# Reordering both hand-written task lists of a fused attention and state-space kernel

## The chip, the cores and the metric

The kernel runs on one core of one Trainium2 chip. The metric is the device time of one execution in microseconds (us). TensorE is PE in the profile (its weight loads are the row PEld), VectorE is DVE, ScalarE is ACT, GpSimd is POOL and SyncE is SP; SP, POOL and, for a few loads, ACT issue the DMAs.

## The reference, cut to what matters

Two layers work on the same input `x` (2048 positions, 640 channels, bf16), and a gate mixes them.

```python
x = A_x
g = _sigmoid((x * gate_w).sum(-1, keepdims=True))
a = _A_ref(x, A_wqkv, A_wo)
b = _B_ref(x, B_A_re, B_A_im, B_B_re, B_B_im, B_C_re, B_C_im, B_log_dt, B_Dskip)
return g * a + (1 - g) * b
```

`_A_ref` is attention of 32 heads of 20 channels over a dilated window: each position sees itself and seven earlier ones at a distance of 2. `_B_ref` builds a convolution kernel `K` of 2048 taps for every channel, as a sum of 192 complex exponentials whose rates come from the parameters (`A`, `B`, `C`, `log_dt`), and convolves `x` with it by a Fourier transform.

## The kernel before, in words

**Tasks and lists.** The work is cut into tasks (class `Task`, L104). `Plan.add` (L123) names a task, the engines that may do it and what it depends on. There are two plans: `main` has 1258 tasks, `tail` 304. Nothing is scheduled at run time: `Plan.order` (L140) reads the sequence from the string in `ORDER` (L54). Every number there is the step from one task's index to the next, and a letter behind it names the engine where the task is not done by the first engine that it allows; most evictions may be done by ScalarE ("A", the default) or by VectorE ("D"). `Plan.emit` (L152) writes the instructions in this sequence and ties each one to the instruction before it on the same engine (L169), so the list fixes the program order of every engine and of every DMA queue, and also the order in which buffers are handed out. The switch of ScalarE's function table (L160) is written where the list changes between exp/ln and sin/atan tasks.

**What is outside the lists.** `SSMParams.build` (from L535) issues the first loads before any task, always in the same sequence on SP: `cre`, `cim`, a first transposed quarter of `x` (`xl[0]`), the Q part of the attention weights (`wl[0]`), `aim`, `are`, the K part and the V part (`wl[1]`, `wl[2]`), then the other three quarters of `x`.

**Projections.** Tasks `late0` to `late59` (L268 to L307) project `x` to Q, K and V: 4 chunks of 512 positions, 3 kinds, 5 pieces. In a chunk, the first five numbers are Q, the next five K, the last five V: `late0` is Q, `late7` is K and `late14` is V of the first chunk. One is 5 matmuls of 512 columns (2 in `late..`, 3 in `late..b`, L284) into a PSUM tile `tb`, of which there are two; `lev..` evicts it (L476 on ScalarE, L478 on VectorE). A third projection therefore waits for the eviction of the first. Attention's `gat` (L424) and `wo` (L448) matmuls use the same two tiles.

**Parameters.** Tasks `wr`, `t0`, `wi`, `tau`, `act_..`, `stt_..`, `mk0` to `mk9` turn the parameters into ten pieces, mostly on VectorE with 960 elements a row (L593 to L630) and some on ScalarE (L602, L658 to L666). The pieces are stored to DRAM (`sp0` to `sp9`, SP, L623) and loaded back as `L` (L734): `L0S` on SP and `L0G` on POOL for the first of ten chunks, `L1` to `L9` on SP for the others. The last piece in both lists is `mk6`.

**Kernel generation.** For chunks 0 to 9: `arg` matmuls (L769), `act` on ScalarE (sine L784, exponential L786; 15 a chunk), `pq` products on VectorE (L806, L808) and `kmm` matmuls (L824). `act00000` is the first of the activations, `pq00` the first of the products. After chunks 4 and 9, `own`, `other` (L872 ff.) spread half of the kernel, which goes through DRAM (`xst`, `xld`) and comes back as `kc` for the first transforms `f1` and `fk`; `fu` transforms `x` (L1272, L1291).

**Attention.** Eight blocks of 256 positions: `prod` (VectorE, L343), `lg`, `max`, `neg`, `exp`, `sum`, `at`, a round trip of the probabilities through DRAM (`ast`, `asb`), `pv` (VectorE, L417), `gat`, `oT`, `wo`, `ga`. `halo` copies (L478) carry the last keys of a block to the next.

**Tail.** The second plan does the second transform step (`fp`, evicted by `sp`), the products (`ta`, `tc`, `Y` on VectorE), the inverse (`inv`, evicted by `cp`; `yp`), the mixing (`tt`, `mx`, `st`) and the stores.

Of the kernel before, what the change touches and what calls it, by code (L numbers as in the profile page):

```python
# [40 lines left out]
def _attn_consts():  # L41
# [10 lines left out]


ORDER = {"main": (  # L54
# [37 lines left out]
), "tail": (  # L92
# [8 lines left out]
)}  # L101


# [1269 lines left out]
```

## Time and profile before

| what | value |
|---|---|
| three runs | 324.24, 324.82, 326.2 us (median 324.82) |
| span of the profiled execution | 324.0 us, 11730 instructions |
| busy PE, DVE, ACT | 278.8, 293.5, 281.6 us |
| bytes moved by DMA | 45.65 MB, mean 141 GB/s |

The profiled execution's time is not listed apart from its span. The page counts an engine as busy while it works on an instruction; what is left of the span is idle. Views that answer for a stretch of the span ("windows") give the busy time of each engine in it and, behind x, the instructions. A row of the timeline begins with the start and the time taken; in square brackets at its end stands how long the engine sat idle before it, and what ended that. A "q" behind an engine's name is its queue of DMA issues.

### The profile page before, as it was taken

What the parts mean: (1) busy time and instruction counts of PE and PEld (TensorE: products, weight loads), DVE (VectorE), ACT (ScalarE), POOL (GpSimd) and SP (SyncE); (2) the same over time, 40 slices, a digit from 0 to 9 for tenths busy, and PEclk for the clock granted to TensorE, in tenths of its full rate; (3) what the DMA queues carried; (4) which work ended last, traced back from release to release, by engine and by line L of the source; (5) the groups of instructions that cost most, each with busy time, mean ns of one, the idle gap of its engine ahead of it and who ended that gap; (6) DMA issues with size and microseconds to landing.
All of it is one profiled execution on the core that took longest, in us unless ns stands there. A gap on an engine that the chain in (4) does not pass through costs nothing. (4 is left out here: it accounts for less than half of the span.)

```text
span 324.0 us, 11730 instructions
## 1 busy us (share of the span) xinstructions
PE 278.8 (86%) x5109; PEld 168.9 (52%) x5134; DVE 293.5 (91%) x408; ACT 281.6 (87%) x425; POOL 55.8 (17%) x87
## 2 busy tenths in 40 slices
PE   0599998999989999999999979889999999996750
PEld 0145443454545545546554544457677776665740
DVE  4888989899998999999999999798999899999891
ACT  1489578999989999999999999799997599997890
POOL 8500027501100000111112202050100000000062
PEclk9998999999999999999999997799999999999995
DMA  8997356642313102467774977144771493963056
GB/s 212 341 223 223 121 172 150 147 96 85 82 39 98 48 7 74 79 166 252 183 183 99 196 160 145 42 125 90 232 270 40 123 320 93 207 127 56 2 141 187
DMA packets 48698, 45.65 MB, mean 141 GB/s; under 512 B 28591, under 2 KB 42483, under 8 KB 48647
## 3 DMA queue, kind: packets, MB, share of 16 engines
q1 hardware_dynamic: 42524, 27.82, 33.4%
q0 software_dynamic: 5216, 16.39, 19.9%
q8 instruction: 40, 0.66, 0.9%
q10 hardware_dynamic: 906, 0.69, 0.7%
q14 instruction: 12, 0.09, 0.1%
HBM read 28.25 MB, written 14.01 MB: 130 GB/s over the span
## 5 line engine op out<-in xcount | busy, mean ns | idle before, releaser
L284 PE MATMUL tb<-bufA 128*128 128x512 bf16 x275 | 74.4, 400 | 6.2 <-DMA bufA<-in_A_wqkv_dram 2.9
L784 ACT ACTIVATE big<-ar 128x740 bf16<-128x740 int16 (+1 forms) x72 | 56.0, 852 | 2.2 <-PE ar L769 1.5
L786 ACT ACTIVATE big<-ar 128x848 bf16<-128x848 f32 x60 | 50.3, 918 | 3.4 <-PE ar L769 3.2
L769 PE MATMUL ar<-Rarg,L 64*128 64x212 bf16 (+4 forms) x600 | 47.5, 255 | 6.5 <-ACT big L784 2.7
L284 PEld LDWEIGHTS <-bufA 128*128 128x128 bf16 x300 | 32.5, 122 | 35.8 <-issue 13.2
L343 DVE TENSOR_TENSOR prod<-qr,kr 128x2048 bf16<-128x2048 bf16 x40 | 47.9, 1220 | 0.9 <-PE lg L349 0.8
L417 DVE TENSOR_TENSOR pv<-vc,asb 128x2048 bf16<-128x2048 bf16 x40 | 47.5, 1217 | 0.2 <-PE tb L424 0.2
L769 PEld LDWEIGHTS <-L 64*128 64x128 bf16 x600 | 22.5, 95 | 35.5 <-issue 32.5
L806 DVE TENSOR_TENSOR pt<-big 128x1024 bf16<-128x1024 bf16 x48 | 32.1, 701 | 1.4 <-PE kps L824 0.8
L824 PE MATMUL kps<-qq,pt 128*32 128x21 bf16 (+1 forms) x2560 | 27.9, 175 | 2.8 <-issue 2.6
L824 PEld LDWEIGHTS <-pt 128*32 128x32 bf16 (+1 forms) x2560 | 23.5, 92 | 11.5 <-issue 9.6
L448 PE MATMUL tb<-wo_sb,oTm 128*128 128x320 bf16 x160 | 27.8, 307 | 0.0
L476 ACT ACTIVATE sp_u<-fp 128x640 bf16<-128x640 f32 x29 | 22.4, 883 | 2.1 <-PE fp L1039 2.1
L476 ACT ACTIVATE sp_k<-fp 128x640 bf16<-128x640 f32 x30 | 22.7, 878 | 1.0 <-PE fp L1039 0.8
L424 PE MATMUL tb<-pv,ind 128*64 128x512 bf16 (+1 forms) x192 | 22.3, 355 | 0.6 <-ACT oTm L476 0.4
L337 POOL DMA_DIRECT2D vc<-vS x16 | 11.6, 728 | 64.0 <-DVE pv L417 57.8
L808 DVE TENSOR_TENSOR qq<-big 128x1344 bf16<-128x1344 bf16 x24 | 21.2, 883 | 0.0
L1039 PEld LDWEIGHTS <-PHI 128*128 128x128 bf16 x160 | 15.6, 97 | 8.1 <-issue 1.5
L448 PEld LDWEIGHTS <-oTm 128*128 128x128 bf16 x160 | 14.7, 99 | 7.8 <-issue 2.8
L160 ACT ACT_TABLE_LOAD x14 | 18.0, 1283 | 0.3
L1157 POOL DMA_DIRECT2D out_dram<-ot x14 | 7.8, 562 | 54.1 <-DVE ot L1139 54.1
L476 ACT ACTIVATE qr<-tb 128x512 bf16<-128x512 f32 (+1 forms) x22 | 10.8, 514 | 6.9 <-PE tb L284 6.9
(152 smaller groups left out, 500.9 us busy)
## 6 DMA issues: line engine op xcount, KB each, us to landing
vc<-vS POOLq DMA_DIRECT2D x16, 327.5 KB, 5.4
vS<-prj POOLq DMA_DIRECT2D x4, 640.0 KB, 5.8
gaS<-ga SPq DMA_DIRECT2D x8, 320.0 KB
Usb<-in_A_x_dram POOLq DMA_DIRECT2D x8, 320.0 KB, 5.2
gaF<-gaS SPq DMA_DIRECT2D x8, 320.0 KB
bufA<-in_A_wqkv_dram SPq DMA_DIRECT2D x3, 800.0 KB
Sprm<-pc SPq DMA_DIRECT2D x10, 240.0 KB
L<-Sprm SPq DMA_DIRECT2D x38, 60.0 KB
```

Of the source, the lines that this page charges most:

```text
L284: nc.tensor.matmul(ppf, self.wq[:, which, kt, e::5], self.xT[:, c0 // 1024, kt, c0 % 1024:c0 % 1024 + SC], start=(kt == 0), stop=(kt == NK ...
L343: nc.vector.tensor_tensor(b[e][:], self.qr[:, sc % NRB, e, :].unsqueeze(1).to_broadcast([128, W, C]), win(self.kr[:, sc % NRB, e, :], 0, W ...
L417: nc.vector.tensor_tensor(o, vw, b["asb"][:].unsqueeze(2).to_broadcast(sh), ALU.mult)
L424: nc.tensor.matmul(b["op", e][64 * a:64 * a + 64, 0:n, :], ind[:, 32:96], b["pv", e][:, w, a, 0:n, :], start=(w == 0), stop=(w == 3), skip ...
L448: nc.tensor.matmul(apf[:, :320], b["oT"][:, e, i * 128:(i + 1) * 128], wo_sb[:, e, hf * 320:(hf + 1) * 320], start=(e == 0), stop=(e == 4))
L476: nc.scalar.activation(o, i, ACT.Identity)
L769: nc.tensor.matmul(ar[:, g2, a0:a0 + ncol], L[rows, gv, sb, l0:l0 + 128], R[rows, c0:c0 + ncol], start=True, stop=True, tile_position=(64 ...
L784: nc.scalar.activation(d_[:, :, s0 * QW:s1 * QW], ar[:].bitcast(I16)[:, :, 0:2 * (s1 - s0) * QW:2], ACT.Sin, scale=SCL)
L786: nc.scalar.activation(dst[:, gp::2].rearrange("p g s n -> p g (s n)"), ar[:, :, 0:2 * EW], ACT.Exp)
L806: nc.vector.tensor_tensor(pt[:, :, k, :], gg[:, :, ::-1] if k else gg, e1, ALU.mult)
L808: nc.vector.tensor_tensor(qq[:], trg[:, :, KI:].rearrange("p a (v m) -> p a v m", v=2), exq[:, :, KI:].unsqueeze(2).to_broadcast([128, 32, ...
L824: nc.tensor.matmul(kps[32 * g:32 * g + 32, h ^ (g // 2), NM * ql:NM * ql + NM], pt[rows, k, v, :], qq[rows, k, v, :], start=(g not in star ...
```

## The change

Only the strings in `ORDER` differ. The tasks, what they compute, their dependencies and the loads ahead of the lists are the same. The diff, cut to the head and the end of each list:

```diff
 ORDER = {"main": (
-    "52 -52 3 -2 3 7 -6 -3 51 -47 6 -5 1 7 -6 45 10 1 2 -1 2 1 -14 1 -43 75 -31 -47 79 -13 -62 76 -65 52 -49 3 -15 62 -55 "
...
-    "-652 1D 640 14 -13D -640 648 -647 1 652D -13 1 -639 1 2 -1D 2 567 -566D 651 1D -651 646 1 1 1 -53 1D 45 1 -25 1D"
+    "94 1 1 -23 -71 80 1 1 -10 1D -75 1 3 7 -8 3 1 54 1 2 1 1 -3D -51 1 119 1 1 -55 -71 1 5 -4 18 -5 -18 11 1 30 33 1 -56 66 "
...
+    "-73 74 -20D 17 10 1D 11 1D -11 1D -12 -642 1 1 1 1 655 1D -65 -589 1 -2 591 49 1 -638 1 565 53 1 -23 1"
 ), "tail": (
-    "0 7 -6 1 1 1D 1 1D 5 -3 4 1 2 1 -7 5D 6 6 8 1D -25 7 124 -114 11 -20 1 2 19 -1 -9 -8 19 1 -10 -9 1 7 2 -5 1 20 1 -14 "
...
+    "0 3 1D 1 1 3 -2 1 2D -9 10 23 -21 23 -24D 2D 6 1 14 2 -7 -13 14 -16 1 2D 4 -20 21 3 1 5 1 5 2 -1 2 -13 -4 1 4 14 1 -25 "
...
```

Read as names, the head of `main` is, engine by engine (a task of the projections' second part, "b", is left out):

| engine | before | after |
|---|---|---|
| PE | late0, 4, 5, 1, 12, 8, 7, 9, 2 | late14, 7, 10, 3, 4, 26, 9, 13, 0 |
| DVE | wr, t1, t0, wr, wi, wi, dtc, tau, near_x1, xl | wi, lev7, wr, t0, wr, t1, wi, dtc, lev3, xl |
| ACT | act_xl, act_ax, act_xa, lnd, lev0, lev4 | lev14, lev10, act_xl, lev4, act_xa, lev26 |
| SP, later | sp9, sp6, L0S, L1, ast0 | sp6, sp9, L1, L0S, ast0 |

(`wr`, `wi`, `tau` and `near_x1` name more than one task; the first `wi` is `cre` times `bim`.) Up to and with `mk6` VectorE's list holds the same tasks before and after, and in addition `lev7`, `lev3` and `prod02` after.

Evictions and copies of `main` that may go either way, ScalarE / VectorE:

| | before | after |
|---|---|---|
| projections (lev) | 49 / 11 | 45 / 15 |
| halo copies | 1 / 6 | 7 / 0 |
| oT | 18 / 6 | 13 / 11 |
| ga | 22 / 10 | 26 / 6 |
| fin | 7 / 3 | 8 / 2 |
| first transforms f1, fk, fu | 34 / 11 | 35 / 10 |

In the tail the counts stay (sp 59 / 5, cp 12 / 8), while three sp and two cp evictions change places each way. The number of table switches in the list is 14 in both.

81 rows, old and new, of the table ORDER are left out of this document.

## The prediction

> **What bounds the kernel now.** I read the page's engine sums first, then the stretches of the span, then the first 65 us of the timeline.
>
> ```profile
> span 324.0 us, 11730 instructions
> PE 278.8 (86%) x5109; PEld 168.9 (52%) x5134; DVE 293.5 (91%) x408; ACT 281.6 (87%) x425; POOL 55.8 (17%) x87
> ```
>
> ```profile
> 4.47:39.84 35.37, 27.77 (x181) 13.67 (x184) 31.70 (x33) 22.61 (x38) 8.34 (x11) 0.95 0.84 235
> 51.24:324.00 272.76, 240.47 (x4867) 150.25 (x4884) 251.74 (x355) 250.63 (x372) 41.00 (x66) 0.97 0.52 129
> 61.50:324.00 262.50, 232.12 (x4784) 146.16 (x4800) 242.45 (x341) 240.41 (x359) 32.96 (x52) 0.97 0.50 127
> 61.50:235.00 173.50, 160.68 (x3800) 92.70 (x3817) 164.77 (x233) 168.28 (x243) 23.85 (x35) 0.98 0.49 119
> 235.00:306.00 71.00, 65.78 (x731) 48.79 (x729) 68.29 (x91) 62.56 (x95) 1.35 (x4) 1.00 0.53 141
> 306.00:324.00 18.00, 5.66 (x256) 4.67 (x256) 9.40 (x19) 9.57 (x23) 7.77 (x14) 0.81 0.56 148
> ```
>
> The columns behind the length are the busy times of PE, PEld, DVE, ACT and POOL. No one engine bounds the kernel: from 61.5 to 235 us VectorE is idle for 8.7 of 173.5 us and ScalarE for 5.2, and from there to 306 us VectorE for 2.7 of 71. What either engine loses at the start has next to no room to be made up later. The slack of both lies at the two ends, so the start deserves the closest reading.
>
> ```profile
> 6.56 0.58 SPq L190 DMA_DIRECT2D bufA<-in_A_wqkv_dram  x1
> 8.87 0.95 SPq L190 DMA_DIRECT2D bufA<-in_A_wqkv_dram  x2
> 11.70 0.16 PEld L284 LDWEIGHTS <-bufA 128*128 128x128 bf16 x2 [3.61 <-DMA bufA<-in_A_wqkv_dram]
> 12.12 0.15 PEld L284 LDWEIGHTS <-bufA 128*128 128x128 bf16 x1 [0.27 <-issue]
> 13.40 0.15 PEld L284 LDWEIGHTS <-bufA 128*128 128x128 bf16 x1 [0.28 <-issue]
> 15.84 0.26 PEld L284 LDWEIGHTS <-bufA 128*128 128x128 bf16 x2 [0.59 <-DMA bufA<-in_A_wqkv_dram]
> 16.38 0.15 PEld L284 LDWEIGHTS <-bufA 128*128 128x128 bf16 x1 [0.28 <-issue]
> 16.81 1.41 PEld L284 LDWEIGHTS <-bufA 128*128 128x128 bf16 x7 [0.28 <-issue]
> 18.45 0.63 PEld L284 LDWEIGHTS <-bufA 128*128 128x128 bf16 x4 [0.23 <-DMA bufA<-in_A_wqkv_dram]
> 14.06 0.60 ACT L476 ACTIVATE qr<-tb 128x512 bf16<-128x512 f32 x1 [1.70 <-PE tb L284]
> ```
>
> Three weight parts are issued one behind the other, and the list before asks for them as they come: TensorE starts with Q at 11.70, meets K at 15.84 (`late5`) and V at 18.45 (`late12`). Weight loads, one a matmul, go 0.43 us apart from 12.12 on and 0.2 us apart from 16.81 (seven in 1.41).
>
> ```profile
> 4.47 1.16 DVE L593 TENSOR_TENSOR wr<-cre,bre 128x960 f32<-128x960 bf16 x1 [3.51 <-DMA bre<-in_B_B_re_dram]
> 23.65 1.16 DVE L630 TENSOR_TENSOR pc<-xa,pc 128x960 bf16<-128x960 f32 x1 [0.77 <-ACT pc L476]
> 24.73 1.15 DVE L630 TENSOR_TENSOR pc<-x,pc 128x960 bf16<-128x960 f32 x1
> 38.68 1.16 DVE L630 TENSOR_TENSOR pc<-t,t 128x960 bf16<-128x960 f32 x1
> 41.97 2.33 SPq L734 DMA_DIRECT2D L<-Sprm  x6
> 50.84 0.53 PE L769 MATMUL ar<-Rarg,L 64*128 64x296 bf16 x8
> 51.24 6.60 ACT L784 ACTIVATE big<-ar 128x888 bf16<-128x888 int16 x9 [1.52 <-PE ar L769]
> 57.86 1.28 ACT L160 ACT_TABLE_LOAD   x1
> 59.65 1.64 ACT L786 ACTIVATE big<-ar 128x848 bf16<-128x848 f32 x2
> 61.50 1.32 DVE L806 TENSOR_TENSOR pt<-big 128x1024 bf16<-128x1024 bf16 x2
> ```
>
> VectorE begins the parameters at 4.47 and ends `mk6`, the last piece, at 39.84. The piece at 23.65 waited 0.77 us for ScalarE, and the next one (24.73), whose inputs had been there for microseconds, did not pass it: a waiting instruction holds its engine. From `mk6` the road goes over DRAM to the first sine at 51.24 and the first product at 61.50.
>
> **The change part by part.**
>
> *First matmul.* The new list opens TensorE with `late14`, a V projection, so the first matmul waits for the third weight part. The loads are issued ahead of the lists and don't change. That part came at 18.45; the first came 5.1 us after its issue, which, added to the third's issue at about 9.35, bounds the landing at 14.5 from below. I take the 18.45 that was seen: TensorE starts 6.75 us later.
>
> *VectorE's queue.* Its second instruction is `lev7`, the eviction of a K projection, ahead of `wr` and the whole parameter work. On TensorE `late14` (5 matmuls), 2 of `late7`, `late10` (5) and the 3 of `late7b` come first, 15 in all. If the slow pace follows the first matmul as before, 11 of them take 0.43 us and 4 take 0.2: 5.5 us, to 24.0. `late10` reuses the tile that `lev14` must empty, but 18.45 + 5 x 0.43 + 0.2 + 0.6 = 21.4 is when `late7` is through too, so nothing is added. Eviction starts some 0.2 us after the last matmul (13.40 + 0.43 against 14.06), and a VectorE eviction takes 0.69:
>
> ```profile
> L478 DVE CAST kr<-tb 128x512 bf16<-128x512 f32 x4 | 2.8, 688 | 0.3 <-PE tb L284 0.3
> L476 ACT ACTIVATE kr<-tb 128x512 bf16<-128x512 f32 x11 | 6.7, 616 | 0.9 <-PE tb L284 0.9
> L343 DVE TENSOR_TENSOR prod<-qr,kr 128x2048 bf16<-128x2048 bf16 x40 | 47.9, 1220 | 0.9 <-PE lg L349 0.8
> ```
>
> So `wr` starts at 24.9 instead of 4.47. Only one product (`wi`) runs ahead. Queued behind `lev7` are all parameter instructions of VectorE, and ScalarE's `act_xl` and `act_xa` wait for those. With the landing at 14.5 all of this would come 3.9 us earlier.
>
> The Trainium skill, "TensorE: Matmul & The Clock Gate", section "What's actually happening", gives about 3.4 us of work before the array runs at full clock; the rows here show the slow spacing for some 4.7 us. By the page's figure three or four of the 15 matmuls would be fast instead of slow, and the estimate would come out about 0.8 us earlier; the trace decides.
>
> *To the last piece.* VectorE was busy 31.7 us from `wr` to the end of `mk6`. The new list has the same work there without that `wi` (1.1), and with `lev3` (0.6 net of overlap) and `prod02` (1.1): 32.3. One wait of 0.3 is in sight: `xl` needs ScalarE's square of `wi` (1.0), with 0.8 of work between. `mk6` ends at 24.9 + 32.3 + 0.3 = 57.5, 17.7 later.
>
> *To the first sine.* SP's first issue of `L` came 2.1 us after `mk6`. Now `L1` (four issues at 2.33 / 6 = 0.39) stands ahead of `L0S` (two): the last issue of `L0S` starts at 57.5 + 2.1 + 5 x 0.39 = 61.6.
>
> ```profile
> L<-Sprm POOLq DMA_DIRECT2D x2, 60.0 KB, 3.1
> ```
>
> 3.1 to landing, as on POOL's queue, makes 64.7, and the matmul ahead of the sine 0.4 (50.84 to 51.24): 65.1, against 51.24. The queue swap has 1.6 us of it. Before, that matmul came 8.5 us behind the start of the last `L0S` issue (42.4), not 3.1, held by what stands ahead of it on TensorE; if that holds it again, 5.4 us are added. I take the landing, since TensorE has 14 us more until then.
>
> *Sum over ScalarE.* From the first sine to the end it was busy 250.6 and idle 22.1 us. The new list leaves it 2.0 more there: 1.0 that stood ahead of it before and 1.0 from evictions that change sides (halo copies and `ga` come, `lev` and `oT` go). 65.1 + 252.6 + 22.1 = 339.8.
>
> ```profile
> L476 ACT ACTIVATE kr<-kr 128x70 bf16<-128x70 bf16 x1 | 0.3, 256 | 0.0
> 315.75 0.69 ACT L1136 ACTIVATE tt<-yp,om 128x320 bf16<-128x320 f32 x1
> 316.47 0.66 DVE L1139 TENSOR_TENSOR ot<-tt,gaF 128x960 bf16<-128x960 bf16 x1 [0.20 <-ACT tt L1136]
> ```
>
> *Sum over VectorE.* Ahead of `pq00` ScalarE has nine sines (6.6), the table (1.28), a halo copy (0.26) and two exponentials (1.64): 65.1 + 9.8 = 74.9, against 61.50. From there 242.4 busy, less 0.7 that moved, and 20.1 idle: 336.6.
>
> *The rest of both lists.* I cost it at nothing: the loads of the engines are the same within 1 us, and the same idle is carried over in the sums. The gain is bounded by that idle, without the ends: 14.5 us on ScalarE (22.1 less the 7.6 behind its last work, from 316.44), 13.2 on VectorE (20.1 less 6.9). The loss is bounded below as the second rival prices it. The tail keeps its counts; VectorE, idle for 2.7 of 71 us there, could gain no more.
>
> The mean of both sums is 338.2 for the span. The runs' median is 324.82 against a profiled span of 324.0, so I add 0.8: **339.0 us**, 14.2 slower.
>
> **The rivals.**
>
> *Half recovered.* The new lists may hold the engines closer together, half of ScalarE's inner idle gone: 65.1 + 252.6 + 7.6 + 7.2 = 332.5, with 0.8 333.3. For it: halo copies leave the busier VectorE. Against: in 61.5 to 235 us only 5.2 us of ScalarE's idle can be had at all, and the rest stands at stage changes.
>
> *Projections held up.* Of the evictions from the two `tb` tiles, four more `lev` and five more `oT` go to VectorE, where each may queue behind a 1.22 us product while TensorE waits for the tile: 9 x 1.22 = 11.0, so 350.0. For it: `lev3` shows the pattern, its tile is kept while four products go first. Against: TensorE has 12.8 us of slack from 61.5 to 235, and four fewer `ga` go there.
>
> *Not slower.* The delay is real, but from 65 us on the lists run almost without a gap: with no inner idle at all ScalarE gives 65.1 + 252.6 + 7.6 + 0.8 = 326.1 and VectorE 74.9 + 241.7 + 6.9 + 0.8 = 324.3. This is within 1% of before only if no more than 2 of 14.5 us of ScalarE's idle are left; below 321.6 it needs the early landing of the V weights as well (3.9 us: 322.2, and even then hardly). ScalarE alone was idle 8.4 of 71 us at the stage changes after 235, which speaks against it.
>
> **How the numbers follow.** Forecast 0.63, half recovered 0.17, held up 0.15, not slower 0.05. The range reaches from between the forecast and the first rival's low side, 331, to just short of the second's price, 349. About 1% (3.2 us) is what a measurement of this kernel can tell from no change: slower by more 0.94, within it 0.04, faster 0.02, the last for a start that I have misread.
>
> **What would show it.** The first matmul of L284 near 18.5; an idle stretch on VectorE of over 15 us, ended by TensorE's `tb`, ahead of `wr` at about 24.9; the last `pc` ending near 57.5; the first sine near 65 and the first `pt` near 75; after that, busy shares of ScalarE and VectorE as before. It would be wrong if `wr` ran before 10 us, if the first sine came before 60, or if ScalarE's idle after the first sine were far from 22 us.

## The result, and the profile after

The kernel after takes 367.44 us (median of 4 runs, 365.11 to 372.79), before in the same session 325.51 us (4 runs, 324.24 to 327.15): 1.126 times as long, interval 1.118 to 1.133, or 42 us slower. The forecast was 339.0 with a range of 331 to 349: the direction was right, the forecast of 14 us more was a third of what came. Ratios here and below leave out the runs that lie over 1.5% above the fastest of their kernel (372.79 here; 352.49 and 353.3, the profiled one, in e1), while the medians in microseconds count every run.

The profiled execution, the shortest of the four, has a span of 363.3 us. VectorE's busy sum on the page of after is that of before within 0.3 us, ScalarE's is 4.5 us larger and TensorE's 12.6; the span has grown by 39.3, so most of it is waiting:

```profile
span 363.3 us, 11751 instructions
PE 291.4 (80%) x5134; PEld 167.4 (46%) x5134; DVE 293.2 (81%) x405; ACT 286.1 (79%) x428; POOL 56.4 (16%) x87
```

The start, from the timeline of after (rows begin with the start and the time taken):

```profile
18.45 0.16 PEld L281 LDWEIGHTS <-bufA 128*128 128x128 bf16 x2 [10.49 <-DMA bufA<-in_A_wqkv_dram]
20.82 0.60 ACT L473 ACTIVATE prj<-tb 128x512 bf16<-128x512 f32 x1 [11.86 <-PE tb L281]
23.10 0.77 PEld L281 LDWEIGHTS <-bufA 128*128 128x128 bf16 x4 [0.23 <-issue]
24.16 0.69 DVE L475 CAST kr<-tb 128x512 bf16<-128x512 f32 x1 [17.11 <-PE tb L281]
24.77 1.15 DVE L590 TENSOR_TENSOR wr<-cre,bre 128x960 f32<-128x960 bf16 x1
56.42 1.16 DVE L627 TENSOR_TENSOR pc<-t,t 128x960 bf16<-128x960 f32 x1
60.36 2.35 SPq L731 DMA_DIRECT2D L<-Sprm  x6
66.21 0.91 ACT L781 ACTIVATE big<-ar 128x888 bf16<-128x888 int16 x1
77.31 0.70 DVE L803 TENSOR_TENSOR pt<-big 128x1024 bf16<-128x1024 bf16 x1
```

TensorE's first projection matmul waits for the third weight part and comes at 18.45, the eviction on VectorE at 24.16 behind 17.11 us of idleness, `wr` at 24.77, the end of `mk6` at 57.58, the first sine at 66.21. Up to here the change costs 15 us (66.21 against 51.24).

From the first sine to the end ScalarE is busy for 255.9 us and idle for 41.2, where the forecast had 252.6 and 22.1; VectorE, from its first product on, is idle for 43.5 us where the forecast had 20.1:

```profile
66.21:363.33 297.12, 252.21 (x4892) 148.77 (x4891) 252.23 (x355) 255.88 (x376) 42.39 (x67) 0.97 0.47 119
77.31:363.33 286.02, 243.52 (x4816) 145.29 (x4815) 242.57 (x341) 245.50 (x362) 37.89 (x60) 0.97 0.46 117
```

The rest is the surprise. I call "the middle" the stretch from the end of the first activation (`act00000`) to the end of `other1`, when the kernel generation is done. Views by stretch, first before, then after (columns behind the length: PE, PEld, DVE, ACT, POOL, each with its instructions, then the granted clock of TensorE, the DMA engines' share and GB/s):

```profile
52.20:227.80 175.60, 161.68 (x3822) 91.77 (x3843) 165.89 (x238) 170.44 (x246) 29.22 (x45) 0.98 0.50 117
```

```profile
67.10:265.20 198.10, 175.15 (x3873) 92.86 (x3874) 171.07 (x244) 176.26 (x252) 30.50 (x46) 0.97 0.46 108
272.40:345.00 72.60, 66.27 (x793) 48.36 (x792) 66.00 (x88) 64.45 (x99) 1.74 (x3) 1.00 0.45 124
345.00:363.30 18.30, 4.12 (x179) 3.22 (x175) 8.60 (x17) 8.38 (x21) 7.74 (x14) 0.75 0.58 145
```

The middle is 22.5 us longer. VectorE's idle time in it goes from 9.7 us (175.60 less 165.89) to 27.0, ScalarE's from 5.2 to 21.8; their work grows by 5 to 6 us, part of it evictions that stood elsewhere before. TensorE's row grows by 13.5 busy and 9.0 idle us; the middle holds 31 more weight loads (3874 against 3843), which before has outside it. The granted clock is nearly the same (0.98 and 0.97). What follows the middle hardly changed. 15 and 22.5 with 2 us of the ends are the 39.3 by which the span grew.

Who waits for whom, in the views of waits of the whole span (us in total, times, longest). Before, then after:

```profile
PEld L769 <- issue: 32.5, 92, 0.8
PEld L284 <- issue: 13.2, 54, 0.5
PEld L824 <- issue: 9.6, 35, 1.5
PEld L349 <- issue: 4.9, 23, 0.4
ACT big L784 <- PE ar L769: 1.5, 1, 1.5
ACT big L786 <- PE ar L769: 3.2, 3, 1.7
PE ar L769 <- ACT big L784: 2.7, 9, 0.5
PE ar L769 <- ACT big L786: 1.1, 4, 0.4
```

```profile
PEld L766 <- issue: 38.7, 98, 1.0
PEld L281 <- issue: 23.5, 70, 3.5
PEld L821 <- issue: 18.3, 53, 2.2
PEld L346 <- issue: 10.8, 28, 3.7
ACT big L781 <- PE ar L766: 11.1, 14, 3.1
ACT big L783 <- PE ar L766: 2.1, 5, 0.8
PE ar L766 <- ACT big L781: 4.8, 11, 0.8
PE ar L766 <- ACT big L783: 4.0, 9, 0.8
```

ScalarE's sines (L784 before, L781 after) wait for their argument tile 14 times instead of once, its exponentials (L786, L783) five times instead of three. The four rows of weight loads that end in "issue" (the profile sees nothing that they wait for) grow from 60.2 to 91.3 us, and their longest from 1.5 to 3.7; in the middle alone they grow from 50.2 to 72.2, since most of what L281 gained lies in the start. One of these stops, in the timeline of after:

```profile
213.69 0.09 PEld L346 LDWEIGHTS <-ind 128*32 128x32 bf16 x1 [3.71 <-issue]
214.00 0.12 PEld L766 LDWEIGHTS <-L 64*128 64x128 bf16 x4 [0.23 <-issue]
214.12 0.69 DVE L362 TENSOR_REDUCE mx<-lg 128x64 f32<-128x512 f32 x1 [3.24 <-PE lg L346]
214.41 0.79 ACT L781 ACTIVATE big<-ar 128x740 bf16<-128x740 int16 x1 [3.06 <-PE ar L766]
...
258.46 0.26 PEld L821 LDWEIGHTS <-pt 128*32 128x32 bf16 x27 [2.20 <-issue]
```

Seven of eight equal weight loads of `lg64` have gone through, and the eighth comes 3.71 us later. VectorE (the maximum of these logits) and ScalarE (the next sine) both run dry, for 3.24 and 3.06 us: here a wait of TensorE is paid at once by both.

### The profile page after: what moved, and what is told of

Same layout as the page of the kernel before. It is cut to its first block, busy times and chain, and to the rows that moved or that the text cites. A ratio compares the mean times of both kernels' runs of the same rounds, so it can differ in the third digit from the quotient of the medians.

```text
span 363.3 us, 11751 instructions
## 1 busy us (share of the span) xinstructions
PE 291.4 (80%) x5134; PEld 167.4 (46%) x5134; DVE 293.2 (81%) x405; ACT 286.1 (79%) x428; POOL 56.4 (16%) x87
## 5 line engine op out<-in xcount | busy, mean ns | idle before, releaser
L281 PE MATMUL tb<-bufA 128*128 128x512 bf16 x300 | 80.9, 406 | 17.9 <-DMA bufA<-in_A_wqkv_dram 9.7
L781 ACT ACTIVATE big<-ar 128x740 bf16<-128x740 int16 (+1 forms) x72 | 56.6, 838 | 11.4 <-PE ar L766 11.1
L766 PE MATMUL ar<-Rarg,L 64*128 64x212 bf16 (+4 forms) x600 | 49.4, 254 | 10.8 <-ACT big L781 4.8
L281 PEld LDWEIGHTS <-bufA 128*128 128x128 bf16 x300 | 32.6, 123 | 51.6 <-issue 23.5
L783 ACT ACTIVATE big<-ar 128x848 bf16<-128x848 f32 x60 | 50.1, 896 | 2.3 <-PE ar L766 2.1
L766 PEld LDWEIGHTS <-L 64*128 64x128 bf16 x600 | 20.8, 95 | 42.5 <-issue 38.7
L821 PE MATMUL kps<-qq,pt 128*32 128x21 bf16 (+1 forms) x2560 | 29.3, 175 | 5.6 <-issue 5.1
L445 PE MATMUL tb<-wo_sb,oTm 128*128 128x320 bf16 x160 | 29.9, 316 | 1.1 <-ACT ga L454 0.8
L473 ACT ACTIVATE prj<-tb 128x512 bf16<-128x512 f32 x18 | 10.9, 605 | 17.1 <-PE tb L281 17.0
L421 PE MATMUL tb<-pv,ind 128*64 128x512 bf16 (+1 forms) x192 | 23.4, 351 | 0.9 <-DVE pv L414 0.6
L473 ACT ACTIVATE sp_u<-fp 128x640 bf16<-128x640 f32 x29 | 23.1, 942 | 1.1 <-PE fp L1036 1.1
L475 DVE CAST kr<-tb 128x512 bf16<-128x512 f32 (+1 forms) x9 | 5.0, 570 | 19.0 <-PE tb L281 19.0
L473 ACT ACTIVATE big<-bp 128x1024 bf16<-128x1024 f32 x18 | 18.1, 1030 | 1.1 <-PE bp L1269 0.7
```

The source lines that it names most:

```text
L281: nc.tensor.matmul(ppf, self.wq[:, which, kt, e::5], self.xT[:, c0 // 1024, kt, c0 % 1024:c0 % 1024 + SC], start=(kt == 0), stop=(kt == NK ...
L421: nc.tensor.matmul(b["op", e][64 * a:64 * a + 64, 0:n, :], ind[:, 32:96], b["pv", e][:, w, a, 0:n, :], start=(w == 0), stop=(w == 3), skip ...
L445: nc.tensor.matmul(apf[:, :320], b["oT"][:, e, i * 128:(i + 1) * 128], wo_sb[:, e, hf * 320:(hf + 1) * 320], start=(e == 0), stop=(e == 4))
L473: nc.scalar.activation(o, i, ACT.Identity)
L766: nc.tensor.matmul(ar[:, g2, a0:a0 + ncol], L[rows, gv, sb, l0:l0 + 128], R[rows, c0:c0 + ncol], start=True, stop=True, tile_position=(64 ...
L781: nc.scalar.activation(d_[:, :, s0 * QW:s1 * QW], ar[:].bitcast(I16)[:, :, 0:2 * (s1 - s0) * QW:2], ACT.Sin, scale=SCL)
```

## The experiments

Ratios are against the kernel before on the same chip (325.1 to 326.9 us there). "Middle" is as above, from each run's profile.

**Where the 42 us lie.**

e1_old_start:

```diff
 main of after:
-its first tasks up to act00000
+the first 160 tasks of before, with their engines, up to act00000
 then what is left, in the order and with the engines of after; tail of after
```

> The changed lists, but main begins with the tasks of the old list up to and with act00000 in their old sequence (160 tasks); the rest follows in the new sequence, the tail is the new one. Theory (two separate costs: a start that comes some 15 us late, and a middle whose sequence feeds ScalarE worse and costs some 24 us whatever the start): about 349 us. Rival (the late start alone throws the rest out of step): back to about 326 us.

Measured 352.05 us, 1.072 (1.061 to 1.083), by the ratio 23 us above before.

e2_new_start:

```diff
 main of before:
-its first tasks up to act00000
+the first 158 tasks of after, with their engines, up to act00000
 then what is left, in the order and with the engines of before; tail of before
```

> The old lists, but main begins with the tasks of the new list up to and with act00000 in their new sequence (158 tasks), the rest in the old sequence, old tail. Theory (two separate costs): about 340 us, 15 above before. Rival (the late start throws the rest out of step): 360 us or more.

Measured 344.33 us, 1.056 (1.050 to 1.063), 18 us above before; 340 was expected. The stretch of the middle in e1, then in e2:

```profile
51.70:253.00 201.30, 176.14 (x3868) 92.87 (x3868) 169.75 (x240) 176.06 (x251) 29.35 (x45) 0.96 0.45 106
```

```profile
68.80:245.10 176.30, 164.30 (x3849) 91.88 (x3848) 166.23 (x239) 171.03 (x248) 29.63 (x46) 0.99 0.50 117
```

The old start leaves a middle of 201.3 us with the new order, the new start one of 176.3 with the old order (before: 175.6). So there are two costs that add up: some 18 us for the start and some 23 for the rest; their sum, 41, is what the whole change costs within 1 us.

**The start.** e5_two_evictions:

```diff
 main of after:
-lev7 on VectorE, lev3 on VectorE
+lev7 on ScalarE, lev3 on ScalarE
```

> The changed lists with two letters changed: lev7 and lev3 on ScalarE, so that nothing of TensorE stands ahead of VectorE's parameter work. If VectorE's block behind lev7 is the whole late start: 352 us, wr near 6 us and the first sine near 51. Theory (ScalarE's act_xl stands behind lev10 and TensorE still starts at 18.45): only part comes back, 358 to 364 us.

Measured 364.28 us, 1.117 (1.109 to 1.124): 3 us less than after, whose interval (1.118 to 1.133) overlaps with this one. `mk6` ends at 54.5 instead of 57.6.

e6_params_first:

```diff
 main of e2, the parameter tasks ahead of the first projection:
+wi wr t0 wr act_xl t1 wi dtc act_xa xl tau near_x1 act_xl tau near_s1 mk0
 late14 late14b lev14 late7 late10 ...
```

> As e2 (new start, old rest), but the parameter tasks from the first wi to mk0 stand ahead of the first projection in the list, so that neither VectorE nor ScalarE stands behind an eviction; TensorE still begins with the V projection. Theory (the blocked queues are most of e2's 18 us, TensorE's late first matmul the smaller part): wr near 5 us, first sine near 55, about 331 us. Rival (TensorE's start at 18.45 alone makes the start late): 340 us or more.

Measured 337.89 us, 1.041 (1.035 to 1.046), 6.4 us less than e2, between the theory's 331 and the rival's 340. `mk6` ends at 51.1. Taking the parameters out from behind the blocked eviction gives back a third of the start's 18 us; two thirds stay. `wr` starts at 7.01 there, but the first projection still waits until 18.46, and before the end of `mk6` VectorE stands idle for 5.45 us ahead of `lev7`, which now comes later, and for 3.88 ahead of an instruction that waits for ScalarE's `ay`.

**The engines.** e3_old_engines:

```diff
 the sequence of after:
-each task on the engine that after gives it
+each task on the engine that before gives it
```

> The new sequence of both lists, but every eviction and copy on the engine that it had before. Theory (the sequence costs, not the sharing): within 5 us of the changed kernel's 367. Rival (evictions on VectorE queue behind products and hold the two tb tiles): 345 to 356 us. In the start lev7 and lev3 go to ScalarE by this, which the theory prices at up to 6 us of the difference.

Measured 389.31 us, 1.192 (1.185 to 1.200). e18_new_letters is the counterpart:

```diff
 the sequence of before:
-each task on the engine that before gives it
+each task on the engine that after gives it
```

> The sequence of before with the choice of engines of after (the counterpart of the sequence after with the engines of before, 389). Theory, sequence and engines of each version fit only each other: 340 or more. Rival, the new shares are neutral or better by themselves and only the sequence costs: 323 to 329.

Measured 351.86 us, 1.082 (1.076 to 1.089). Sequence and engines fit only each other: the old pair takes 325, the new pair 367, the mixed ones 389 and 352. For e3 neither the theory (within 5 us of 367) nor the rival (345 to 356) came. Evictions on VectorE (the second rival of the prediction) are not what the new sequence suffers from; with the old choice of engines it is 22 us worse.

**Spread or local.** e17_splice_middle:

```diff
 main:
+before up to pq42c (633 of 1258 tasks)
+then what is left, in the order and with the engines of after; tail of after
```

> The main list of before up to the product pq42c (633 of 1258 tasks), then the rest in the order and with the engines of after, and the tail of after. Behind the old start the new sequence was 8.9 us late at pq42c and 25.2 at the end of other1. Theory, the loss is spread over the sequence and each half keeps its own: 325 + 16.3 less 1 for the tail = 340 (336 to 345). Rival, one early misplacement in the first half throws the rest out of step: 325 to 330.

Measured 341.92 us, 1.050 (1.045 to 1.054), 16 us above before, as the second half alone was seen to lose (16.3). So this half loses its share behind an undisturbed first half, and the loss is not the echo of one early misplacement.

**Single places of the middle.** Four edits of after, each at a wait that its profile shows:

```diff
 e8_args_sooner, main of after:
-69 of the 150 arg tasks where after has them
+each 1 to 7 places sooner in TensorE's order (2.8 on average)
 e9_rows_paced:
-rows paced by kmm600 kmm620 kmm700 kmm710 kmm720 kmm810 kmm820
+rows paced by kmm700 kmm713 kmm723 kmm800 kmm803 kmm813 kmm820
 e10_f15_sooner, main of after:
-... wo510 f15 own1 other1 f1e5 ...
+... fue1 f15 f1e5 vc1792 ...
 e19_ready_first, main of after:
-15 VectorE instructions behind one that waits (such as pv40b behind max6)
+the same 15 ahead of it
```

> The changed lists, but 69 of the 150 arg tasks moved forward in TensorE's order until no more than 0.5 us of TensorE's work stands between the activation that empties their tile and them. Theory (ScalarE runs dry because arg matmuls stand behind projections and kmm groups): ScalarE's waits for ar fall from 13 us to under 6, and the time by 6 to 15 us. Rival (TensorE is simply short of time, so that what is moved ahead makes something else late): within 4 us of 367.

Measured 387.66 us, 1.189 (1.181 to 1.197), 20 us worse than after, where the theory had 6 to 15 less and the rival no change. The waits point to why. In e8:

```profile
PE ar L767 <- ACT big L782: 13.1, 24, 1.9
PE ar L767 <- ACT big L784: 10.1, 23, 1.1
ACT big L782 <- PE ar L767: 7.1, 10, 2.2
```

ScalarE's waits for sine arguments fall from 11.1 to 7.1 us, and TensorE's for a free argument tile rise from 8.8 to 23.2. There are two `ar` tiles: an argument too late stops ScalarE, one too early stops TensorE and what is queued behind it.

> The changed lists, but the loads rows1 to rows7 (320 KB each) wait for later kmm tasks (kmm700, 713, 723, 800, 803, 813, 820), so that they don't come in one burst with the vc loads near 200 to 210 us. Theory (in the burst TensorE's instruction page comes late, which stops it for 3.8 us inside lg64 and 2.3 us inside kmm922): the stop inside lg64 is under 1.5 us, and the time 2 to 6 us shorter. Rival (these stops are something else): they stay, time within 2 us of 367.

Measured 368.80 us, 1.131 (1.123 to 1.139): nothing. The stop in `lg64` shrinks from 3.7 to 2.2 us, not under the theory's 1.5, and others grow.

> The changed lists, but the last first-transform of the first half, f15, and its eviction stand 14 tasks of TensorE earlier, ahead of fin9, so that own1 on VectorE, which must wait for it, has no wait. Theory (VectorE's 3.3 us before own1 lie on the chain): 2 to 3.5 us shorter, 364. Rival (slack on the way to the second half's kernel hides it): within 1 us of 367.

Measured 363.84 us, 1.117 (1.109 to 1.125): 3.6 us less than after, where the theory put it, though the intervals overlap.

> The sequence after, with 15 instructions of VectorE moved one to three places ahead on VectorE: at each place where VectorE stood idle for 0.4 us or more in the middle (18.7 of its 26.2 us there) for one instruction while a later one of its own list had all its inputs, the later one now goes first. TensorE's, ScalarE's and the queues' orders and all engines are those of after. Theory: the new list is out of step with the times at which things get ready, and an engine that works in order loses at such places; the moved instructions fill the gaps, at most 18.7 us, less what the displaced ones now come later (15 x about 0.5): 354 to 361 instead of 367. Rival: TensorE is the late one whatever stands in VectorE's list, and the wait comes back one instruction later: 364 to 371.

Measured 368.78 us, 1.123 (1.111 to 1.135): nothing. 18.7 of VectorE's 26.2 idle us stood ahead of an instruction that could have been passed, and passing it gained nothing: VectorE is idle for 29.9 us in the middle where after has 27.0, so the waits came back behind the moved instructions.

**TensorE's changes of tile shape.** Between weight loads of different tile shapes the row of weight loads has a gap; in the view of weight loads before, a run with 128x128 tiles of 512-column matmuls and then another shape:

```profile
70.39 0.98 PEld L284 LDWEIGHTS <-bufA 128*128 128x128 bf16 x5
71.77 0.30 PEld L769 LDWEIGHTS <-L 64*128 64x128 bf16 x8 [0.41 <-issue]
72.23 0.29 PEld L381 LDWEIGHTS <-ident 128*128 128x128 bf16 x8 [0.15 <-issue]
```

0.41 us one way, 0.15 the other. Counted from the first sine to some 8 us behind the middle, before has 250 such changes with 52.2 us of gaps, after 296 with 62.0; in the middle alone it is 243 with 50.6 and 290 with 60.6. Not all of this is lost: the matmuls of earlier loads run on in these gaps, and in the middle of before TensorE's matmul row is idle for only 13.9 us (175.60 less 161.68). e11_fewer_switches and e12_before_regrouped put equal shapes side by side:

```diff
 e11, main of after:    54 TensorE tasks moved by at most three places in TensorE's order
 e12, main of before:   32 TensorE tasks moved by at most three places in TensorE's order
```

> The sequence after, with 54 TensorE tasks between the first argument matmul and the end of main moved by at most three places in TensorE's own order, nearly always beside a task whose weight tile has the same shape. Engines, VectorE's, ScalarE's and the queues' orders are those of after. Theory: a change of the weight tile's shape stops TensorE (128*128 to 64*128 or 128*32: mostly 0.40 us, others 0.03 to 0.2), and after has 296 of them in the middle, 62.0 us of gaps, where before has 250 and 52.2. The moves take the changes from 304 to 240 by tasks and the gaps down by an estimated 18 us; not all of it lies on the path, so about 355 (349 to 361) instead of 367. Rival, the gaps only fill time in which TensorE would wait anyway: 365 to 370.

> The same regrouping on the sequence before: 32 TensorE tasks moved by at most three places, changes of shape from 255 to 230, gaps down by an estimated 9.5 us. Theory: TensorE is on the path for less of the middle there, so some 3 us come back: 322.5 (319 to 324.5), faster than both kernels. Rival, TensorE's gaps are covered in this sequence or the moved tasks arrive too late for their readers: 325 to 329.

Measured 376.35 us, 1.157 (1.152 to 1.162), and 331.91 us, 1.020 (1.016 to 1.024). In e11 the gaps did fall, to 46.7 us at 219 changes, and the kernel became 9 us slower; in e12 they fell to 45.1 at 224, and it became 7 us slower. Both times neither the theory nor the rival's range came. The waits of e11 again:

```profile
ACT big L782 <- PE ar L767: 12.7, 9, 6.0
PE ar L767 <- ACT big L782: 10.0, 21, 0.9
PE ar L767 <- ACT big L784: 8.2, 16, 1.1
```

TensorE's waits for argument tiles doubled (8.8 to 18.2). Here the order of the tasks counted for more than the gaps at changes of shape.

**TensorE's amount of work.** e15_light_projections and e16_light_before (both leave out part of Q, K and V, as the expectations say):

```diff
 matmuls of the projections, positions 1024 to 2047, four of five:
-nc.tensor.matmul(ppf, ..., self.xT[..., c0 % 1024:c0 % 1024 + SC], ...)
+nc.tensor.matmul(ppf[:, 0:64], ..., self.xT[..., c0 % 1024:c0 % 1024 + 64], ...)
```

> The sequence after, with work left out: in the projections of positions 1024 to 2047 four of the five matmuls of each piece do 64 instead of 512 columns, so Q, K and V are incomplete there; instructions, evictions and all other work stay. A matmul of 512 columns takes TensorE about 0.2 us, so some 18 us of TensorE's work leave the middle (30 pieces x 4 x 0.15). Theory A, TensorE's own work sets the middle of the new sequence: 356 or less instead of 367. Theory B, the middle is set by engines that wait in turn for single instructions placed late, and TensorE has time to spare: 363 to 368.

> The sequence before with the same work left out (four of five matmuls of each projection piece of positions 1024 to 2047 at 64 columns). Theory A: TensorE is not what sets the middle there, so at most 3 us come off: 322 to 325. Theory B: the same 322 to 325; only the difference between this and the run on the sequence after tells the theories apart.

Measured 362.52 us, 1.110 (1.103 to 1.117), and 326.02 us, 0.998 (0.995 to 1.001). The middle of e15, then of e16:

```profile
67.30:261.20 193.90, 165.72 (x3875) 92.03 (x3874) 171.38 (x244) 174.92 (x253) 30.45 (x46) 0.89 0.47 110
```

```profile
51.10:226.40 175.30, 149.53 (x3844) 90.11 (x3844) 165.76 (x238) 169.94 (x247) 30.06 (x46) 0.97 0.50 117
```

In before 12 us less of TensorE's time (161.68 to 149.53) are worth nothing; in after 9 us less (175.15 to 165.72) are worth 4 to 5. The time of e15 lies 0.5 us below the second theory's range and 6.5 above the first's, so TensorE's amount of work is hardly the bound. The granted clock of e15's middle was 0.89 instead of 0.97, which may have eaten part of what was left out, so more than 5 us cannot be excluded.

**The stops at fixed instruction numbers.** The 3.7 us stop in `lg64` stands inside a run of equal instructions, and nothing that the profile shows ends it. Counting the records of the row PEld from the start (weight loads and the few waits of its sequencer), the longest stops of this kind come at 100 to 102 modulo 128. A load and its matmul are two instructions, so that is about every 256. The page has 40 packets of instructions in 0.66 MB for TensorE's 10,268 instructions:

```profile
q8 instruction: 40, 0.66, 0.8%
```

One packet for 257 of them. If the stop is the fetch of the next packet, it has to stay at its number when the list is shifted. e13_shifted:

```diff
 late13 late0 late5 late2 late6 late1 late8 late11 of after, ahead of the first matmul:
+for _ in range(8): nc.tensor.matmul(ppf[:, 0:16], ...)
```

> The sequence after, with 8 extra small matmuls (16 columns, overwritten by the real ones) ahead of each of 8 projections of the first chunk, so that every later weight load has a number 64 higher. Theory: the stops of 1 to 4 us inside a run of equal weight loads come at fixed numbers (100 to 102 modulo 128 as the trace counts them), so they stay at these numbers and leave the logits in which 3.8 us were lost and the products with 1.1, 1.4 and 2.3; others appear 64 loads earlier in the list. Rival: the stops belong to these tasks, and the same tasks stop again for 3 to 4 and 2 us. For the time: 64 small matmuls of 0.1 us cost the start 2 to 4 us; the sum of the stops over 0.8 us, 15.1 in the middle, may go to 6 to 16, so 360 to 372 by the theory, 369 to 372 by the rival.

Measured 366.62 us, 1.130 (1.124 to 1.136). In its weight loads `lg64` now runs through at 213.33, and other tasks stop for 2.9 us, in the middle of equal loads:

```profile
212.05 0.45 PEld L825 LDWEIGHTS <-pt 64*32 64x32 bf16 x49 [2.94 <-issue]
213.33 0.14 PEld L350 LDWEIGHTS <-ind 128*32 128x32 bf16 x8 [0.36 <-issue]
...
256.04 0.52 PEld L825 LDWEIGHTS <-pt 64*32 64x32 bf16 x55 [2.87 <-issue]
```

Their numbers are again 100 to 102 modulo 128: the stops belong to the instruction's number and not to the task. Their sum in the middle (from one load's start to the next, those over 0.5 us at 98 to 102) is 14.2 us, in after 14.4, in before 4.3, and the time is the same as after's within 1 us. Some of them are changes of shape at such a number; without these the sums are 11.9, 11.8 and 3.2. So the run moved the stops and left open what they cost.

What they wait for can be read in the traces, which have a time for every packet of q8. In after, a packet of 16 KB moves from 210.84 to 212.27, while TensorE stands, and `lg64` goes on at 213.69, 1.42 us later; DMA is busy then (share 1.08, 197 GB/s from 209.7 to 213.6). All nine stops of over 1 us at these numbers in the middles of before, after and e13 end 1.2 to 1.5 us behind the end of such a packet, and in after no load at such a number, counted in order with the packets, comes sooner than 1.2 us behind the end of its packet. So these long stops are waits for instructions, as far as times can show it.

For their price, e20_stops_in_before holds TensorE on purpose:

```diff
 before, ahead of the first logits of a block:
+for _ in range({(6, 0): 14, (7, 0): 10}.get((sc, e), 0)):
+    nc.tensor.matmul(b["lg"][0:32], ind[:, 0:32], b[e][:, :, 0:64], start=True, stop=True, ...)
```

> The kernel before, with 14 extra matmuls of 512 columns ahead of the first logits of attention block 6 and 10 ahead of those of block 7 (overwritten by the real ones): TensorE is held for some 3.0 and 2.2 us there, like the two longest stops at fixed instruction numbers in the profile after (3.7 and 2.2 us). Theory: such a stop is paid nearly in full, because ScalarE and VectorE run out of input in it: 328.5 to 331. Rival: TensorE's slack covers it: 324.5 to 327.

Measured 346.67 us, 1.061 (1.056 to 1.067). The edit did more than the expectation says: `sc` has its last value, 7, when these instructions are written, so all eight blocks got 10 matmuls, 80 in all, as the profile of e20 shows:

```profile
L349 PEld LDWEIGHTS <-ind x80: 92/97/97, 25.0 to 221.8; 128*32 128x32 bf16 x80
```

Each group of ten held TensorE for 1.7 to 2.0 us (ahead of block 7 from 220.0 to 222.0), 15 us in all, and the kernel grew by 20.5. Six of the eight and a part of a seventh lie in the middle, some 12 us, and the middle grew by 20.5 too (196.1 against 175.6). The stops at fixed numbers grew with it, from 4.3 us to 10.2. So time lost on TensorE at these places is paid in full and more; what it gains (e16) is worth nothing. Because the added matmuls stand ahead of the logits, e20 also delays the attention of every block, which it does not tell apart from TensorE's lost time.

**A mixed tail.** e14_tail_mix:

```diff
 before; tail:
+after's tail up to cp19
 then what is left, in the order of before
```

> The main list of before, the tail list of after up to its last cp, then the order of before for the mixing and the stores. Theory: up to the first cp the tail after ran about 1 us quicker than before's, and its end 2.3 us slower, so the mix gives 324.4, 1 us below before. Rival: the lead came from later inputs that were all there, not from the order: 325.5 or more.

Measured 325.89 us, 1.002 (0.998 to 1.005): no difference, as the rival said. No version that beats the kernel before was found.

## Why the prediction was wrong

*First matmul, VectorE's queue, the last piece: right.* Forecast 18.45, 24.0 (with `wr` at 24.9) and 57.5; measured 18.45, 24.16 (`wr` 24.77) and 57.58. The slow spacing of weight loads lasted from 18.45 to about 23.1, 4.65 us, as in the rows of before and longer than the 3.4 us weighed there.

*First sine and first product: right in kind, short by 1.1 and 2.4 us.* Forecast 65.1 and 74.9, measured 66.21 and 77.31. SP's issues of `L` began 2.8 us behind `mk6` instead of 2.1 (60.36), and the sines, put at 9.8 us with what follows them, took 11.1; one wait of 0.69 us for an argument stands between them.

*The price of the start: right in kind, short by 4 us.* The forecast makes the change a delay of 14 us; e2, which has the new start alone, costs 18 and would lie inside the range.

*"The rest of both lists. I cost it at nothing": this is the step that failed.* It was mis-sized at 0 where the runs show 23 us (e1; 22.5 in the middle of after's profile). ScalarE's idle time after the first sine was carried over as 22.1 us, and VectorE's after the first product as 20.1, on the argument that the engines' loads are the same; measured are 41.2 and 43.5. The loads are the same within 3.3 us, and the idle time is not a property of the loads: in the middle it went from 9.7 to 27.0 us on VectorE and from 5.2 to 21.8 on ScalarE, with 5 to 6 us more work. The prediction itself names idle time far from 22 us on ScalarE as what would make it wrong.

*The bound of that step failed too.* The loss was bounded by nine evictions of 1.22 us on VectorE (the second rival). e3 shows that these evictions are not a cost of the new sequence, and the true loss was twice as large. What was not looked for is the other direction: how close the two engines stood to running dry in before. The waits of before show it as one wait for sine arguments and three for exponentials in the whole run, 4.7 us; with two `ar` tiles little can be stored ahead. That this tightness is why the new order loses is argued, not shown.

*What the middle's 22 us are.* Shown: they belong to the rest of the sequence (e1, e2), the second half has its part without the first (e17), they are not the choice of engines alone (e3, e18), and they were not taken back by these moves of VectorE's waiting instructions (e19), of TensorE's tasks beside tasks of equal shape (e11) or of arguments ahead (e8); both lists lose when TensorE's order is moved by a few places (e11, e12); holds of TensorE ahead of the logits are paid in full (e20).

The traces also show TensorE's gaps at changes of shape 10 us larger in the middle and its stops at fixed numbers 10.1 (14.4 against 4.3), which looks like the 22. This sum does not carry the loss. The two overlap, matmuls run in the first, and the matmul row's idle time grows by only 9.0. In e11 the gaps were taken away, and the kernel became slower. e18 is the clearest case: its middle is 15.8 us longer than before's, with 243 changes and 50.5 us of gaps as before and 5.2 us of stops against 4.3:

```profile
53.00:244.40 191.40, 166.25 (x3846) 92.77 (x3846) 167.70 (x239) 171.20 (x248) 28.68 (x44) 0.98 0.45 107
```

VectorE and ScalarE lose 23.7 and 20.2 us there, nearly as much as in after, and e8 is 20 us slower than after with half its stops (7.4). Otherwise the stops go with the order: 2.5 to 5.0 us in the five runs with the middle of before, 10.2 to 16.2 in ten with the middle of after or a few moves in it (but for e8), 11.0 in e17, and 10.2 in e20, where the old order was held up. What stays open is how the new order loses its 22 us: every edit at a single place was either without effect or worse, but for 3.6 us in e10 and 3 in e5, which the intervals do not separate from nothing.

*The rivals.* "Half recovered" and "not slower" expected that the new lists hold the engines closer together; the opposite came. "Held up" had the right sign for the rest and the wrong mechanism.

## What to carry to other kernels

When a hand-written order is replaced, the delay at the start can be worked out from the rows of before (here the last piece to 0.1 us, the whole start to 4), but the idle time of the stretch behind it must not be carried over: in a kernel whose engines are 94 and 97% busy in a stretch, this is a property of the order, and more likely the best than the middle of what another order gives. Every reordering of the middle of before here (e12, e17, e1) made it slower, by 7 to 23 us. So give the range room on that side: here the loss was 22 us in a stretch in which TensorE, the third engine, had 13.9 us of slack. A wait with a later ready instruction behind it looks like a loss of the order on that engine; before reordering it, ask whether what it waits for would have come sooner.

## What the runs showed of the hardware

- At every 256th instruction or so TensorE can stop inside a run of equal instructions: up to 3.7 us in after, 6.3 in e11, 1.5 in before, most of them under 0.5 us. The stops move with the instruction's number (e13), their sum grew in a TensorE that was held up (4.3 to 10.2 us, e20), and the nine of over 1 us in before, after and e13 end 1.2 to 1.5 us behind a 16 KB packet of instructions.
- At a change of the weight tile's shape the row of weight loads has a gap: mostly 0.40 us from 128*128 or 128*64 to 64*128, 0.17 behind 64*128, 0.03 behind 64*32 (medians in the middles of before and after); 243 and 290 such gaps are 50.6 and 60.6 us, in part covered by running matmuls.
- In before, removing 12 us of TensorE's work from the middle gained nothing (e16), and holding it for 15 us ahead of the logits cost 20 (e20).
